# Attention and spectral mixing: the last mode groups moved between loop and tail, and the last sixteen modes scattered row by row

## The chip, the cores and the metric

The kernel runs on one core of a Trainium2 chip. The metric is device time in microseconds from launch to end, the median of several runs. The profile shows one execution of its own; the time from its first to its last instruction is called the span.

The engines are PE (matrix products and transposes), DVE (vector), ACT (scalar functions and copies), POOL (GpSimd) and SP (issues transfers). POOL and SP each have a queue of DMA transfers of their own, and both use the same 16 DMA engines.

## The reference

Inputs in float32: q, k, v of shape (8 batches, 8 heads, 576 positions, 64), w_phi (64 x 128), and for the second half w_r and w_i (64 modes x 512 x 512 each) and w_ch (512 x 512).

```python
# 1. linear attention with a Hedgehog feature map
def phi(x):
    proj = x @ w_phi
    proj = proj - max(abs(proj), axis=-1)
    return concat([exp(proj), exp(-proj)], axis=-1)
kv  = einsum('bhsf,bhsd->bhfd', phi(k), v)
z   = sum(phi(k), axis=2)
num = einsum('bhsf,bhfd->bhsd', phi(q), kv)
den = einsum('bhsf,bhf->bhs', phi(q), z) + 1e-06
x   = num / den                      # as (batch, position, head * 64 + d)
# 2. spectral mixing
X = rfft(x, axis=1)                  # the first 64 modes are used
Yr = Xr @ w_r - Xi @ w_i             # per mode m: (512) @ (512 x 512)
Yi = Xr @ w_i + Xi @ w_r
u = x + irfft(Y)
out = u + relu(u @ w_ch)
```

The 134 MB of w_r and w_i are read once and cast to bfloat16 on the way by the transfers themselves.

## The kernel before

**First part, a loop of 32 + 2 iterations (L577 to L654).** Iteration n works on stage n: two heads of one batch, or one head of two batches. It is a software pipeline: features and maxima of the current stage, key-value products `kv_mm` and numerators of the stage before, and `x_mm`, the forward Fourier transform as products with cosines and sines, of the stage before that. The result of the transform lies in XT0 or XT1. `vscale` (L278) multiplies V on POOL by exponentials `ee` that ACT makes from the maxima of this iteration. All of it is written in the order of issue by hand (`tc.manual_schedule()`), and each engine runs its own instructions in that order.

**The mode groups.** The products with w_r and w_i are split into 32 groups of 2 MB after the cast (`groups`, L108): a group k >= 8 is a quarter of the 512 input features (g = 1, 2, 3) and eight modes (gi = 0 to 7). Each has four loads of 512 KB, two of w_r and two of w_i, issued from POOL (L166). Three groups have buffers (`NW = 3`), so the loads of group k are issued after the products of group k-3. `weights(k)` puts the four issues on the list `due`, and `issue_weights(n)` takes up to n from it. In iterations 4 to 8 up to four loads are issued and V is scaled afterwards (before iteration 4, V comes first); from iteration 9 it scales V first and issues three, from 27 on four.

The list `at` (L548) says after which iteration `mode_mm` multiplies the next group: group 16 after iteration 27, 17 after 29, 18 after 30 and 19 after 31. `mode_sum` adds the group into Yacc at the start of the next iteration (L453), and for g = 3 into a bfloat16 tile `yst` (L462) instead.

**Second part, the tail (L816 to L851).** It begins with group 20. Beside the remaining groups it does for all pairs of blocks of x: `flip_x` (8 transposes on PE into PSUM tag T3, a copy sT on DVE) and `times_w` (products with w_ch, `psW`, tag T2, copied to xw on ACT), as the list `plan` spreads them by `pieces`. `reordered` puts rows of x in another order. For groups 24 to 31, the last input features, yst is transposed (ptY, tag T3) to sY, and after every second of them `by_batch` makes both z, the product of sY with w_ch, and the modes themselves with rows of one batch together: 64 products of 32 columns of sY into T0 and T1. ACT and DVE copy eight pieces of 32 rows to `zy`, whose halves are called zall and yall. For the last pair (groups 30 and 31) only batches 0 and 4 are copied directly; the other six go through a bfloat16 tile `st` and six transfers of 64 KB, two from SP and four from POOL.

**Third part, 20 output units (L873 to L888).** A unit is two blocks of 128 positions (four units are half as large). `add_xw` and `add_z` sum x w_ch and the inverse transform of z in a PSUM tile psB, ACT takes the Relu (L793); `add_x` and `spec` sum x and the inverse transform of the modes in psA, DVE adds the two (L807). For 11 units marked late, POOL adds x instead (L811). SP sends the result (L888). Units take the tags T2 and T3, or T0 and T1, in turn. The psB of the first unit is begun before group 31's products, its psA after group 31's transposes.

PSUM is claimed by tags: a tile of a tag waits until the readers of the tile before it in that tag are done.

Of the kernel before, what the change touches and what calls it, by code (L numbers as in the profile page):

```python
# [10 lines left out]
F32 = mybir.dt.float32  # L11
F32R = mybir.dt.float32r
BF16 = mybir.dt.bfloat16
# [13 lines left out]
def kernel(  # L27
# [379 lines left out]
                             start=(dc == 0), stop=(dc == 3))  # L407
        nc.scalar.copy(xw0[:, i, :], ps)

    def mode_mm(k, tag="yr"):  # L410
        g, gi = groups[k]
        XT = XTs[1 - g if k < 8 else g % 2]
        wt = W.pop(k)
        if gi < 0:
            psY = psum.tile([128, 2, DMODEL], F32, name="psY2", tag="pC", bufs=1)
            for par in range(2):
                for ri in range(2):
                    for j in range(4):
                        for x in range(2):
                            r = slice(64 * x, 64 * x + 64)  # L420
                            m = 16 * (-1 - gi) + 8 * x + 2 * j + par
                            c0 = (16, 0, 48, 32)[2 * ri + par]
                            nc.tensor.matmul(
                                psY[32 * j:32 * j + 32, x, :],
                                lhsT=XT[r, c0:c0 + 32, m],
                                rhs=wt[ri][r, 2 * j + par, :],
                                start=(par == 0 and ri == 0), stop=(par == 1 and ri == 1),
                            )
            return psY
        psY = psum.tile([128, DMODEL], F32, name="psY", tag=tag, bufs=1)  # L430
        for ri in range(2):
            for i in range(2):
                for j in range(4):
                    nc.tensor.matmul(  # L434
                        psY[32 * j:32 * j + 32, :],
                        lhsT=XT[:, 16 + 32 * ri:48 + 32 * ri, 32 * i + 4 * gi + j],
                        rhs=wt[ri][:, 2 * j + i, :],
                        start=(i == 0 and ri == 0), stop=(i == 1 and ri == 1),
                    )
        return psY  # L440

    def mode_sum(k, psY, pb=None):
        g, gi = groups[k]
        if gi < 0:
            G = -1 - gi
            if g == 0:
                nc.vector.tensor_copy(Yacc[:, 2 * G:2 * G + 2, :], psY)
            else:
                nc.vector.tensor_tensor(
                    out=Yacc[:, 2 * G:2 * G + 2, :], in0=psY, in1=Yacc[:, 2 * G:2 * G + 2, :],  # L450
                    op=ALU.add)
        elif g < 3:
            nc.vector.tensor_tensor(  # L453
                out=Yacc[:, gi, :], in0=psY, in1=Yacc[:, gi, :], op=ALU.add)
        else:

            cuts = [0, DMODEL] if k < 31 else [0, DMODEL // 2, DMODEL]
            yst = []
            for a, b in zip(cuts, cuts[1:]):
                t = pb.tile([128, b - a], BF16, name="yst", tag="yst" if k < 31 else f"yst{a}",  # L460
                            bufs=2 if k < 31 else 1)
                nc.vector.tensor_tensor(out=t, in0=psY[:, a:b], in1=Yacc[:, gi, a:b], op=ALU.add)  # L462
                yst += [t[:, x:x + 128] for x in range(0, b - a, 128)]
            return yst


# [78 lines left out]

    psY = None
    k_in = k_out = 0
    at = [5, 6, 7, 8, 9, 10, 12, 13, 17, 18, 19, 20, 21, 23, 24, 25, 27, 29, 30, 31]  # L548
    pa_last_cm = None
    with tc.manual_schedule():  # L550
        load(S[0], "qk")
# [25 lines left out]
        for n in range(N + 2):  # L577
# [110 lines left out]
        nc.vector.tensor_copy(sT, pt)  # L688
        ahead.append((i, sT))

    def times_w():
        i, sT = ahead.pop(0)
        ps = psum.tile([128, 2, DMODEL], F32, name="psW", tag="T2")
        for x in range(2):
            for dc in range(4):
                nc.tensor.matmul(ps[:, x, :], lhsT=sT[:, x, dc, :], rhs=wchb[:, dc, :],  # L696
                                 start=(dc == 0), stop=(dc == 3))
        nc.scalar.copy(xw[:, i - N_EARLY:i + 2 - N_EARLY, :], ps)  # L698

    def pieces(n):  # L700
        for _ in range(n):
            if todo:
                flip_x(todo.pop(0))
            if copies:
                copies.pop(0)()
            if len(ahead) > 1:
                times_w()
            if copies:
                copies.pop(0)()
# [18 lines left out]
    def by_batch(sY, P):  # L728
# [19 lines left out]
        def copy(j, h, eng):  # L748
            eng(zy[rows, :, j + 4 * h, :], ps[h][32 * j:32 * j + 32])

        if P < 3:
            for h in range(2):
                mm_z(h)
                mm_r(h)
            copies.extend([lambda j=j: (copy(j, 0, nc.scalar.copy),
                                        copy(j, 1, nc.vector.tensor_copy)) for j in range(4)])
            return

        for h, eng in ((0, nc.scalar.copy), (1, nc.vector.tensor_copy)):
            mm_z(h)
            mm_r(h)
            copy(0, h, eng)
            st = pb.tile([128, 2, DMODEL], BF16, name=f"st{h}", bufs=1)
            eng(st, ps[h])
            for j in range(1, 4):
                (nc.sync if j == 1 else nc.gpsimd).dma_start(
                    zy[rows, :, j + 4 * h, :], st[32 * j:32 * j + 32])

    def parts(u):
# [37 lines left out]
            nc.gpsimd.tensor_tensor(out=o, in0=o, in1=xs_all[:, i:i + 2, :], op=ALU.add)  # L811


    u0 = dict(bc=((0, 0), (0, 1)), half=False, late=False, tags=("T2", "T3"))

    with tc.manual_schedule():  # L816
        plan = {20: 3, 21: 3, 22: 2, 23: 2, 24: 1, 25: 1, 26: 1, 27: 1, 28: 1, 29: 1, 30: 1, 31: 0}
        while k_out < 32:
            k = k_out
            gi = groups[k][1]  # L820
            while k_in < min(k_out + NW, 32):
                weights(k_in)
                k_in += 1
            issue_weights()
            if k == 31:
                add_xw(u0)
            yst = mode_sum(k, mode_mm(k, "T3"), pb)
            k_out += 1
            if yst is not None:
                if ahead:  # L830
                    times_w()
                if gi % 2 == 0:
                    sY = pb.tile([128, 4, 2, 128], BF16, name="sY", tag="sY")
                for a, b, tag in ((0, 4, "T3"),) if k < 31 else ((0, 2, "T0"), (2, 4, "T1")):
                    pt = psum.tile([128, b - a, 128], BF16, name="ptY", tag=tag)
                    for dc in range(a, b):
                        nc.tensor.transpose(pt[:, dc - a, :], yst[dc], ident_b)
# [81 lines left out]
```

## Time and profile before

| what | value |
|---|---|
| time, median of 3 runs | 454.23 us (453.52 to 456.52) |
| time of the profiled execution | 453.88 us |
| its span | 452.1 us |
| PE, DVE, ACT, POOL busy | 314.2, 293.5, 270.1, 218.5 us |
| queue q0 (POOL) | 76.75 MB, 94.8% of 16 engines' span |
| queue q1 (SP and others) | 20.19 MB, 13.0% |
| read from and written to HBM | 163.64 MB, 9.44 MB |
| mean granted PE clock | 0.863 |

The page of the profile lists busy times, then the span in 40 slices of 11.3 us with the busy share in tenths, the DMA queues, the chain of work that ended last, the costliest groups of instructions, and the DMA issues. Other views give single instructions in order of time (start, duration, engine, line, operation, output <- inputs, count, and in brackets the idle time before and what ended it), or the busy time of each engine in chosen windows: after each window's length come five pairs of busy us and instructions (PE, weight loads of PE, DVE, ACT, POOL), then the granted PE clock, the busy share of the DMA engines and the GB/s that landed. PEld is the loading of PE's weights. The span is 1.8 us shorter than the same execution's time.

### The profile page before, as it was taken

What the parts mean: (1) busy time and instruction counts of PE and PEld (TensorE: products, weight loads), DVE (VectorE), ACT (ScalarE), POOL (GpSimd) and SP (SyncE); (2) the same over time, 40 slices, a digit from 0 to 9 for tenths busy, and PEclk for the clock granted to TensorE, in tenths of its full rate; (3) what the DMA queues carried; (4) which work ended last, traced back from release to release, by engine and by line L of the source; (5) the groups of instructions that cost most, each with busy time, mean ns of one, the idle gap of its engine ahead of it and who ended that gap; (6) DMA issues with size and microseconds to landing.
All of it is one profiled execution on the core that took longest, in us unless ns stands there. A gap on an engine that the chain in (4) does not pass through costs nothing.

```text
span 452.1 us, 11841 instructions
## 1 busy us (share of the span) xinstructions
PE 314.2 (69%) x4980; PEld 209.1 (46%) x4997; DVE 293.5 (65%) x418; ACT 270.1 (60%) x552; POOL 218.5 (48%) x303
## 2 busy tenths in 40 slices
PE   3475677677848777666858766665788868677993
PEld 2364465565626655444635644442444534243341
DVE  6578879987858788866756877752322263454873
ACT  4575787885746868765846866652344552353662
POOL 3955558394554744844535652460222322200893
PEclk9987989986676679988686789886999988799998
DMA  6999999999999999999999999999999999992697
GB/s 179 195 229 219 201 219 218 229 218 218 224 226 216 227 221 221 219 222 221 234 221 220 222 223 211 177 198 211 211 211 211 210 211 211 211 210 52 234 337 300
DMA packets 60612, 97.75 MB, mean 216 GB/s; under 512 B 3920, under 2 KB 28752, under 8 KB 60560
## 3 DMA queue, kind: packets, MB, share of 16 engines
q0 software_dynamic: 51920, 76.75, 94.8%
q1 hardware_dynamic: 8480, 20.19, 13.0%
q8 instruction: 39, 0.64, 0.5%
q14 instruction: 13, 0.11, 0.1%
q10 hardware_dynamic: 160, 0.07, 0.1%
HBM read 163.64 MB, written 9.44 MB: 383 GB/s over the span
## 4 chain that ended last, share of the span: by engine, by line
DMA 29%; PE 24%; DVE 22%; ACT 13%; issue 5%; POOL 5%; SPq 1%; DVEq 0%; ACTq 0%; POOLq 0%
DMA wi<-in_moe_w_i_dram 28%; DVE mkq L245 7%; DVE xs_all L348 4%; PE psW L696 4%; ACT AA L252 3%; DVE nd L334 3%; PE psY L434 3%; ACT e L274 2%; DVE tB L327 2%; PE psNB L317 2%; PE kvz L298 2%; ACT AA L256 2%; POOL vaug L282 2%; PE psWe L406 1%; ACT kvzF L307 1%
## 5 line engine op out<-in xcount | busy, mean ns | idle before, releaser
L282 POOL TENSOR_TENSOR vaug<-vn,ee 128x576 bf16<-128x576 f32 x64 | 72.8, 1158 | 99.8 <-ACT ee L267 94.5
L252 ACT ACTIVATE AA<-psT 128x1024 bf16<-128x1024 f32 x64 | 62.0, 1021 | 25.7 <-PE psT L220 25.1
L256 ACT ACTIVATE AA<-psk 128x1024 bf16<-128x1024 f32 x64 | 61.4, 1009 | 0.0
L274 ACT ACTIVATE e<-mkq 64x4 f32<-64x4 f32 (+1 forms) x128 | 26.3, 206 | 58.5 <-DVE mkq L245 56.1
L166 POOL DMA_DIRECT2D wr<-in_moe_w_r_dram x48 | 30.1, 633 | 57.9 <-PE psY L434 45.4
L698 ACT CAST xw<-psW 128x1024 bf16<-128x1024 f32 x17 | 17.2, 1012 | 48.3 <-PE psW L696 48.3
L166 POOL DMA_DIRECT2D wi<-in_moe_w_i_dram x48 | 30.3, 640 | 22.4 <-DMA wi<-in_moe_w_i_dram 12.9
L245 DVE TENSOR_REDUCE mkq<-psk 128x8 f32<-128x1024 f32 x32 | 38.8, 1213 | 3.2 <-PE psk L211 3.1
L245 DVE TENSOR_REDUCE mkq<-psq 128x8 f32<-128x1024 f32 x32 | 39.0, 1217 | 0.3
L696 PE MATMUL psW<-wchb,sT 128*128 128x512 bf16 x129 | 34.5, 406 | 4.5 <-ACT xw L698 3.4
L202 DVE COPY kT<-ptr 128x640 bf16<-128x640 bf16 x32 | 15.7, 492 | 29.9 <-PE ptr L196 29.9
L317 PEld LDWEIGHTS <-AA 128*128 128x128 bf16 x640 | 31.2, 115 | 8.3 <-issue 7.8
L298 PE MATMUL kvz<-vaug,AA 64*128 64x65 bf16 x1152 | 30.1, 213 | 5.3 <-POOL vaug L287 3.8
L434 PEld LDWEIGHTS <-XT 128*32 128x32 bf16 x384 | 16.1, 167 | 37.8 <-DMA wi<-in_moe_w_i_dram 18.9
L327 DVE TENSOR_TENSOR tB<-psNB,e 128x650 f32<-128x650 f32 x32 | 26.7, 834 | 10.4 <-PE psNB L317 9.6
L220 PE MATMUL psT<-qT,w 64*128 64x512 bf16 x64 | 15.0, 456 | 24.4 <-DVE mkq L245 24.3
L453 DVE TENSOR_TENSOR Yacc<-psY,Yacc 128x512 f32<-128x512 f32 x16 | 11.0, 689 | 31.9 <-PE psY L434 31.8
L298 PEld LDWEIGHTS <-AA 64*128 64x128 bf16 x1152 | 25.7, 109 | 9.8 <-issue 6.5
L348 DVE TENSOR_TENSOR xs_all<-nd,rden 128x640 bf16<-128x640 f32 x32 | 28.8, 900 | 1.1
L196 PE MATMUL ptr<-ident_b,k 128*128 128x128 bf16 x160 | 19.2, 271 | 14.6 <-DVE qT L202 11.3
L334 DVE TENSOR_TENSOR nd<-psNA,tB 128x650 f32<-128x650 f32 x32 | 26.7, 835 | 3.8 <-DVE tB L327 0.5
L434 PE MATMUL psY<-wi,XT 128*32 128x512 bf16 x192 | 17.8, 441 | 16.3 <-DMA wi<-in_moe_w_i_dram 16.3
(134 smaller groups left out, 737.9 us busy)
## 6 DMA issues: line engine op xcount, KB each, us to landing
wr<-in_moe_w_r_dram POOLq DMA_DIRECT2D x64, 512.0 KB, 13.6
wi<-in_moe_w_i_dram POOLq DMA_DIRECT2D x64, 512.0 KB, 15.2
out_dram<-of SPq DMA_DIRECT2D x16, 512.0 KB, 3.6
vn<-in_v_dram SPq DMA_DIRECT2D x24, 288.0 KB, 6.1
q<-in_q_dram POOLq DMA_DIRECT2D x12, 288.0 KB, 11.2
k<-in_k_dram POOLq DMA_DIRECT2D x12, 288.0 KB, 12.4
vn<-in_v_dram SPq DMA_DIRECT2D x16, 144.0 KB, 4.8
out_dram<-Yacc SPq DMA_DIRECT2D x8, 128.0 KB, 2.8
```

What stands on the lines that cost most here:

```text
L166: nc.gpsimd.dma_start(t.rearrange("p (m i) e -> p m (i e)", i=2), w[8 * gi + y:8 * gi + 8:2, g * 128:(g + 1) * 128, :].rearrange("m (p i) ...
L245: nc.vector.tensor_reduce(out=o, in_=i, axis=AX.X, op=ALU.max, apply_absolute_value=True)
L252: nc.scalar.activation(AA[:, 0, ab, 0:1024].rearrange("f (x j p) -> f j x p", j=2, p=64), st["psT"].rearrange("f j (x p) -> f j x p", p=64 ...
L256: nc.scalar.activation(AA[:, 1, ab, 0:1024].rearrange("p (c j f) -> p j c f", c=4, j=2), st["psk"], ACT.Exp, scale=sc)
L282: nc.gpsimd.tensor_tensor(out=vaug[:, ab, :, 0:64], in0=st["v"], in1=ee[:, ab, :].unsqueeze(2).to_broadcast([128, 9, D_]), op=ALU.mult,)
L298: nc.tensor.matmul(kvz[:, hh, ab * 65:(ab + 1) * 65], lhsT=AA[r, 1, ab, 128 * j:128 * j + 128], rhs=vaug[r, ab, j, :], start=(j == 0), sto ...
L317: nc.tensor.matmul(p[:, hh, 65 * c:65 * c + 65], lhsT=AA[:, 0, ab, x:x + 128], rhs=kvzF[:, hh, ab * 65:(ab + 1) * 65], start=True, stop=True,)
L327: nc.vector.tensor_tensor(out=tB, in0=st["psNB"], in1=e2.unsqueeze(3).to_broadcast([128, 2, NCH, 65]), op=ALU.mult,)
L334: nc.vector.tensor_tensor(out=nd, in0=st["psNA"], in1=st["tB"], op=ALU.add)
L348: nc.vector.tensor_tensor(out=xo, in0=nd[:, :, :, 0:64], in1=rden.to_broadcast([128, 2, NCH, 64]), op=ALU.mult,)
L434: nc.tensor.matmul(psY[32 * j:32 * j + 32, :], lhsT=XT[:, 16 + 32 * ri:48 + 32 * ri, 32 * i + 4 * gi + j], rhs=wt[ri][:, 2 * j + i, :], st ...
L696: nc.tensor.matmul(ps[:, x, :], lhsT=sT[:, x, dc, :], rhs=wchb[:, dc, :], start=(dc == 0), stop=(dc == 3))
```

## The change

Four things change together.

1. *Attachment.* Group 17 is multiplied after iteration 28, 18 after 29, 19 after 30, and group 20, formerly the first of the tail, after 31. The tail begins with group 21, and `plan` spreads its pieces over one group fewer.
2. *Order of issue.* From iteration 9 on, two loads are issued ahead of V's scaling and two behind it.
3. *The last sixteen modes.* `by_batch` serves the first three pairs only. For groups 30 and 31 `by_row` sends the rows of yst to yall and those of z to zall, seven batches by transfers of 16 rows (16 KB), two on SP and five on POOL each time. `z_of_group` makes z of one group with four products; `first_batch` makes batch 0 of both groups directly.
4. *Order at the end and PSUM tags.* The copies of the third pair are all issued in iteration 29 of the tail. Two `times_w` and the first unit's `add_x` stand between group 31's products with w_r and those with w_i; two flips without products stand behind group 30. The units use T2 and T1, or T0 and T3, so that T3 and T0 serve the last groups' products and are free again for the second unit.

```diff
-    at = [5, 6, 7, 8, 9, 10, 12, 13, 17, 18, 19, 20, 21, 23, 24, 25, 27, 29, 30, 31]
+    at = [5, 6, 7, 8, 9, 10, 12, 13, 17, 18, 19, 20, 21, 23, 24, 25, 27, 28, 29, 30, 31]
...
-            if 9 <= n < N:
-                vscale(cur)
...
-            issue_weights(3 if 9 <= n < 27 else 4)
+            issue_weights(4 if n < 9 else 2)
             if n in (1, 3):
                 load_qk((n + 5) // 2)
-            if 4 <= n < 9:
+            if 4 <= n < N:
                 vscale(cur)
+            if n >= 9:
+                issue_weights(2)
...
-    def pieces(n):
+    def pieces(n, keep=1):
...
-            if len(ahead) > 1:
+            if len(ahead) > keep:
                 times_w()
...
+    def by_row(all_b, t, gi):
+        for b in (4, 1, 5, 2, 6, 3, 7):
+            (nc.sync if b in (4, 1) else nc.gpsimd).dma_start(
+                all_b[16 * gi:16 * gi + 16, b, :], t[b::8, :])
+
+    def first_batch(sY):
+        cols = [sY[:, dc].rearrange("p g c -> p (g c)")[:, 0::8] for dc in range(4)]
+        ps = psum.tile([128, 2, DMODEL], F32, name="psZY", tag="T0")
+        r = slice(96, 128)
+        for dc in range(4):
+            nc.tensor.matmul(ps[r, 0, :], lhsT=cols[dc], rhs=wchb[:, dc, :],
+                             start=(dc == 0), stop=(dc == 3))
+        for dc in range(4):
+            nc.tensor.matmul(ps[r, 1, dc * 128:(dc + 1) * 128], lhsT=cols[dc], rhs=ident_b,
+                             start=True, stop=True)
+        nc.scalar.copy(zall[r, 0, :], ps[r, 0, :])
+        nc.vector.tensor_copy(yall[r, 0, :], ps[r, 1, :])
+
+    def z_of_group(sY, gi):
+        ps = psum.tile([128, DMODEL], F32, name="psZ", tag="T3")
+        for dc in range(4):
+            nc.tensor.matmul(ps, lhsT=sY[:, dc, gi % 2, :], rhs=wchb[:, dc, :],
+                             start=(dc == 0), stop=(dc == 3))
+        z = pb.tile([128, DMODEL], BF16, name="z8", tag="z8")
+        nc.scalar.copy(z[:, 0:256], ps[:, 0:256])
+        nc.vector.tensor_copy(z[:, 256:512], ps[:, 256:512])
+        by_row(zall, z, gi)
...
-        plan = {20: 3, 21: 3, 22: 2, 23: 2, 24: 1, 25: 1, 26: 1, 27: 1, 28: 1, 29: 1, 30: 1, 31: 0}
+        plan = {21: 3, 22: 3, 23: 2, 24: 2, 25: 1, 26: 1, 27: 1, 28: 1, 29: 1, 30: 2, 31: 0}
...
+            psY = mode_mm(k, "T3", ris=(0, 1) if k < 31 else (0,))
             if k == 31:
+                times_w("T2")
+                times_w("T0")
+                add_x(u0)
+                mode_mm(k, ris=(1,), psY=psY)
                 add_xw(u0)
-            yst = mode_sum(k, mode_mm(k, "T3"), pb)
+            yst = mode_sum(k, psY, pb)
             k_out += 1
             if yst is not None:
+                if gi >= 6:
+                    by_row(yall, yst, gi)
                 if ahead:
                     times_w()
...
-                if k == 31:
-                    add_x(u0)
-                if gi % 2 == 1:
+                if gi == 7:
+                    first_batch(sY)
+                if gi >= 6:
+                    z_of_group(sY, gi)
+                elif gi % 2 == 1:
                     by_batch(sY, gi // 2)
-            pieces(plan[k])
+            pieces(plan[k], 2 if k == 30 else 1)
+            while copies and k == 29:
+                copies.pop(0)()
...
-            if k == 30:
-                times_w()
...
-            u["tags"] = ("T2", "T3") if n % 2 == 0 else ("T0", "T1")
+            u["tags"] = ("T2", "T1") if n % 2 == 0 else ("T0", "T3")
```

More of the change, by code (lines that the diff above doesn't have):

```diff
@@ L408, in times_w_early, with mode_mm @@
         nc.scalar.copy(xw0[:, i, :], ps)
-    def mode_mm(k, tag="yr"):
+    def mode_mm(k, tag="yr", ris=(0, 1), psY=None):
         g, gi = groups[k]
         XT = XTs[1 - g if k < 8 else g % 2]
-        wt = W.pop(k)
+        wt = W[k]
         if gi < 0:
@@ L429, in mode_mm @@
             return psY
-        psY = psum.tile([128, DMODEL], F32, name="psY", tag=tag, bufs=1)
-        for ri in range(2):
+        if psY is None:
+            psY = psum.tile([128, DMODEL], F32, name="psY", tag=tag, bufs=1)
+        for ri in ris:
             for i in range(2):
@@ L455, in mode_sum @@
         else:
+            yst = pb.tile([128, DMODEL], BF16, name="yst", tag="yst", bufs=3)
             cuts = [0, DMODEL] if k < 31 else [0, DMODEL // 2, DMODEL]
-            yst = []
             for a, b in zip(cuts, cuts[1:]):
[L460 to L463, printed above, removed]
+                nc.vector.tensor_tensor(out=yst[:, a:b], in0=psY[:, a:b], in1=Yacc[:, gi, a:b],
+                                        op=ALU.add)
             return yst
@@ L689, in flip_x, with times_w @@
         ahead.append((i, sT))
-    def times_w():
+    def times_w(tag="T2"):
         i, sT = ahead.pop(0)
-        ps = psum.tile([128, 2, DMODEL], F32, name="psW", tag="T2")
+        ps = psum.tile([128, 2, DMODEL], F32, name="psW", tag=tag)
         for x in range(2):
@@ L749, in copy @@
             eng(zy[rows, :, j + 4 * h, :], ps[h][32 * j:32 * j + 32])
[L751 to L761, printed above, removed]
+        for h in range(2):
             mm_z(h)
             mm_r(h)
[L764 to L769, printed above, removed]
+        copies.extend([lambda j=j: (copy(j, 0, nc.scalar.copy),
+                                    copy(j, 1, nc.vector.tensor_copy)) for j in range(4)])
+    def by_row(all_b, t, gi):
[23 more added lines that the diff above has]
+        by_row(zall, z, gi)
     def parts(u):
@@ L811, in spec @@
             nc.gpsimd.tensor_tensor(out=o, in0=o, in1=xs_all[:, i:i + 2, :], op=ALU.add)
-    u0 = dict(bc=((0, 0), (0, 1)), half=False, late=False, tags=("T2", "T3"))
+    u0 = dict(bc=((0, 0), (0, 1)), half=False, late=False, tags=("T2", "T1"))
     with tc.manual_schedule():
-        plan = {20: 3, 21: 3, 22: 2, 23: 2, 24: 1, 25: 1, 26: 1, 27: 1, 28: 1, 29: 1, 30: 1, 31: 0}
+        plan = {21: 3, 22: 3, 23: 2, 24: 2, 25: 1, 26: 1, 27: 1, 28: 1, 29: 1, 30: 2, 31: 0}
         while k_out < 32:
@@ L833 @@
                     sY = pb.tile([128, 4, 2, 128], BF16, name="sY", tag="sY")
-                for a, b, tag in ((0, 4, "T3"),) if k < 31 else ((0, 2, "T0"), (2, 4, "T1")):
+                for a, b, tag in ((0, 4, "T3"),) if k < 31 else ((0, 2, "T0"), (2, 4, "T3")):
                     pt = psum.tile([128, b - a, 128], BF16, name="ptY", tag=tag)
                     for dc in range(a, b):
-                        nc.tensor.transpose(pt[:, dc - a, :], yst[dc], ident_b)
+                        nc.tensor.transpose(pt[:, dc - a, :], yst[:, dc * 128:(dc + 1) * 128],
+                                            ident_b)
                     nc.vector.tensor_copy(sY[:, a:b, gi % 2, :], pt)
-                if k == 31:
-                    add_x(u0)
-                if gi % 2 == 1:
+                if gi == 7:
[3 more added lines that the diff above has]
+                elif gi % 2 == 1:
                     by_batch(sY, gi // 2)
-            pieces(plan[k])
+            pieces(plan[k], 2 if k == 30 else 1)
+            while copies and k == 29:
+                copies.pop(0)()
             if k <= 24 or k % 2 == 0:
```

## The prediction

> **What bounds the kernel now.** I read first the page's slices, then the groups with their releasers, then windows where the slices dip, and last the timeline from the final weights on.
>
> ```profile
> DMA  6999999999999999999999999999999999992697
> ...
> q0 software_dynamic: 51920, 76.75, 94.8%
> ...
> wi<-in_moe_w_i_dram POOLq DMA_DIRECT2D x64, 512.0 KB, 15.2
> ```
>
> The 16 DMA engines are full from the second slice to the 36th, and GpSimd's queue (q0), which carries the weights, holds them for 94.8% of the span. So up to about 411 us the kernel is a stream of weights; an engine's work counts only if it delays a load, or comes after the last one. The stream has one real hole:
>
> ```profile
> core 0: us, PE busy (x) PEld busy (x) DVE busy (x) ACT busy (x) POOL busy (x), PEclk, DMA share, GB/s
> 282.00:284.00 2.00, 1.41 (x53) 1.19 (x50) 1.79 (x3) 1.89 (x3) 0.00 (x0) 1.00 1.12 210
> 284.00:286.00 2.00, 1.76 (x45) 1.51 (x43) 1.45 (x3) 1.98 (x6) 1.37 (x2) 1.00 1.05 199
> 286.00:288.00 2.00, 0.31 (x4) 0.31 (x3) 1.76 (x3) 1.62 (x5) 2.00 (x4) 0.93 0.59 114
> 288.00:290.00 2.00, 1.62 (x13) 0.78 (x13) 1.57 (x2) 0.00 (x0) 1.47 (x3) 0.50 0.86 137
> 290.00:292.00 2.00, 2.00 (x24) 0.78 (x24) 0.10 (x2) 1.41 (x5) 0.00 (x0) 0.72 1.07 197
> ...
> 298.00:300.00 2.00, 1.48 (x13) 0.94 (x14) 1.40 (x3) 0.09 (x1) 1.94 (x4) 0.50 1.12 164
> 300.00:302.00 2.00, 2.00 (x19) 0.77 (x17) 0.53 (x1) 1.28 (x5) 0.00 (x0) 0.66 1.05 188
> ```
>
> The last column is what landed; 211 GB/s is the steady rate of weights alone. In the timeline the first load that ends the hole is issued at 286.98, behind the scaling of V (L282), which had waited for ACT.
>
> After the last load, the timeline:
>
> ```profile
> 402.98 0.69 DVE L462 TENSOR_TENSOR yst<-psY,Yacc 128x512 bf16<-128x512 f32 x1
> ...
> 409.56 0.68 PE L434 MATMUL psY<-wr,XT 128*32 128x512 bf16 x8
> 411.45 0.69 PE L434 MATMUL psY<-wi,XT 128*32 128x512 bf16 x8 [1.21 <-DMA wi<-in_moe_w_i_dram]
> ...
> 418.50 1.22 DVE L807 TENSOR_TENSOR of<-psA,of 128x1024 f32<-128x1024 f32 x1
> ```
>
> For group 31 PE waits for the load, not the load for PE: everything that could be done before has been done by 411.45, with 1.2 us to spare. From there 40.7 us remain, nearly all of them the 20 output units; PE is busy 9.8 of 10 us in them, so they shift as a block with the moment at which they can run freely.
>
> **The change, part by part.** Starts and durations are those of the profiled execution (span 452.1, its own time 453.88, against a median of 454.23).
>
> *Attachment and order of issue.* Group 17's product moves from iteration 29 to 28, 18 to 29, 19 to 30, 20 from the tail to 31. A group's product frees the buffers of the group three later, so group 20's loads can be issued one iteration earlier, at about 272 to 277 instead of 286.98, and two of the four now stand before V's scaling, where POOL idles 5.07 to 6.91 us for ACT. The lost bytes are, window by window, (12+97+74+14+47+23) GB/s x 2 us = 534 KB, at 211 GB/s **2.5 us**. Bounds: 0, if the hole reappears elsewhere; 3.5, if the smaller dips before it go too. I take 2.5, the measured hole: the loads of 17, by the order of the stream, have landed when iteration 28 ends (the queue, filled up to the issue at 277.06, ran dry near 286; two groups of 10 us earlier is 266, iteration 28 ends at 270). The two issues cost 2 x 0.64 = 1.28 us of POOL per iteration, covered by that idle time; without the cover V's scaling would be 1.28 us later, and behind it wait the second pair of loads and the kv products, which had 3.4 us of room (copy of ee done at 259.2, first product at 262.56). An issue can also wait for an older load: rows of the tail show 1.6 to 2.2 us for each. That needs a full queue, so it delays compute but starves nothing. Cost taken: 0. Group 20's product (1.5 us of PE) and sum (0.69 us of DVE) enter iteration 31, beside the loads.
>
> *The last products after the last load.* Removed: by_batch for the last pair, 64 small matmuls (413.64 to 416.08, 2.4 us of PE), four evictions (1.0 and 1.0 on ACT, 1.22 and 1.23 on DVE) and six transfers of 64 KB. Added after the load: first_batch (4 products of 512 columns by 0.215 = 0.86, 4 of 128 columns about 0.25), z_of_group (4 x 0.215 = 0.86), evictions of half size, and 14 transfers of 16 KB, four on SP, ten on POOL (0.55 each, 5.5 us, done before POOL's first addition L811). From the start w of the last wi product: sums and transposes as before, second copy of sY done w+2.2, first_batch done w+3.4, its two evictions w+4.0, z half copies w+4.8, Relu of the first unit w+4.9 to 5.9, first L807 at w+5.9. Before, it was 418.50 - 411.45 = 7.05, because DVE was held by two evictions of 1.2 us. The third unit needs batch 4 by transfer: issued w+4.85 on SP, landing 2.1 us later (the median of the six st transfers; 1.9 to 2.2), w+7.0, a stall of 0.2 us. The second unit finds T0 and T3 free, where T0 and T1 had to wait for st. Net **-1.2 us**, bounds -1.5 and -0.4 (if rows of 16 KB land a microsecond later). The Trainium skill, "DMA: Bandwidth & Descriptors", section "Bandwidth", speaks against the split: transfers under 64 KB are dominated by descriptors and should be batched. By the fit under "Anatomy of one DMA" a 16 KB row would be estimated at 2.04 us against 2.15 for 64 KB, so the sum by it is the same to 0.1; the 64 KB rows here agree with 1.9 to 2.2 us.
>
> *Between the last two groups.* This is the term that I think decides. Before, group 30 did one flip and one product with w_ch; now its step holds the group's z product, two flips, then group 31's wr product, two products with w_ch and add_x, all in PE order ahead of the wi product. Let L be the landing of group 30's wi (401.0 before); 31's lands at L+10. All four pairs of copies of by_batch(2) now run in iteration 29. Before, two ran (400.50 to 402.95) and yst began at 402.98 = L+2.0. Two more of 1.22 put it at L+4.4; if the products of group 29 run at full clock (they ran at half: psW 3.6 instead of 1.9, psZY started late) some 2.3 us less, L+2.1. Then, strictly in turn between PE and DVE: yst 0.69, ptY 0.40, sY 0.42, z 1.0, its copy 0.42, flip 0.61, sT 0.69, flip 0.61, sT 0.69, nine hand-overs of 0.05: 6.0. Then wr 0.5, two psW of 8 x 0.215 = 1.73 back to back, add_x 0.43: 4.4. The wi product starts at L+12.5 to L+14.8 at full clock, **2.5 to 4.8 us after its load**, where before it was 0. T0 and T2 are ready by then. On top comes the clock. The views by windows show what follows a thin one:
>
> ```profile
> 366.22:369.63 3.41, 1.28 (x15) 0.89 (x15) 2.21 (x4) 3.02 (x3) 1.05 (x2) 1.00 1.12 210
> 369.63:373.04 3.41, 2.44 (x16) 0.68 (x18) 1.46 (x2) 1.85 (x2) 0.79 (x2) 0.50 1.12 211
> ...
> 386.70:390.11 3.41, 1.21 (x10) 0.36 (x9) 2.81 (x3) 1.95 (x2) 0.87 (x2) 1.00 1.12 210
> 390.11:393.52 3.41, 2.44 (x12) 0.84 (x13) 0.69 (x1) 0.00 (x0) 0.61 (x1) 0.50 1.12 211
> ```
>
> PE busy 1.2 or 1.3 us of 3.41 was followed by a granted clock of 0.50 for two windows. The alternation above has PE busy 0.40 + 1.0 + 0.61 in about 5 us, as thin; the two psW would then take up to 7 us for 3.5. Bounds: 2.5 (early, full clock) and 9.0 (late, and 4.2 for products at half clock). I take **+5.1**: between the two full-clock ends (3.6), and about a third of what the clock can add (1.5), because a half-clock group 29 leaves the next step no idle time and so a full clock at its start. The Trainium skill, "TensorE: Matmul & The Clock Gate", Part 1, says that the clock falls after at least one idle window of about 3.4 us. Read strictly it would not fall here, and the sum would be 1.5 lower, 453.8. This trace is against that strict reading: 1.21 us busy sufficed.
>
> **Sum:** -2.5 + 5.1 - 1.2 = +1.4; 453.88 + 1.4 = **455.3 us**.
>
> **Rivals.**
> 1. *Full clock through the last two groups.* Wait 2.5 to 4.8, middle 3.6: -2.5 + 3.6 - 1.2, 453.8 us (452.7 to 455.0). For it: 400.35 to 414 ran at full clock. Against it: the new order thins PE there. It is also what the page on the clock gate gives when read strictly.
> 2. *Nothing of it binds.* If group 30's chain is overtaken by nothing and the two psW fit into the wait for the load, as they are placed, the whole gain stays: 453.88 - 2.5 - 1.2 = 450.2 us. For it: PE had 1.2 us spare at 411.45. Against it: the chain above is longer than the 10 us between two groups.
> 3. *Slower: half clock over both psW.* The wait becomes 9.0 and the first units start cold: -2.5 + 9.0 - 1.2 = +5.3, 459.2 us. It decides from a wait of 3.7 on, since below that the gains outweigh it. For it: the thin windows above; against it: PE has to fall cold exactly in that step.
> 4. *The loop doesn't do what it says.* POOL waits before V's scaling for older loads, kv products slip, the hole moves: 0 gained, 5.1 lost, 1.2 gained, 457.8 us. For it: POOL waited 9.6 us for loads at L166 before 270 already; against it: those waits come with a full queue.
>
> **How the numbers follow.** Forecast, half clock for part of that step, 0.42 (waits from 4 to 8, 454.2 to 458.2); rival 1 0.24, rival 2 0.08, rival 3 0.17, rival 4 0.09. The range 451.0 to 459.8 leaves out rival 2 and the upper half of rival 3. About 1% is what a measurement of this kernel can tell from no change: 449.7 to 458.8. Below lies a part of rival 2, 0.06; above most of rival 3 and the upper edges of rival 4 and the forecast, 0.21; within, 0.73.
>
> **What would show it.** Right: no window under 200 GB/s between 284 and 302; loads end near 409; the last wi product starts several us after its load, released by PE's own order, with PE thin in the 6 us behind group 30's psW and perhaps a clock of 0.50; first L807 some 5.9 us after that product. Wrong: a last wi product released by its load (rival 2), a new hole (rival 4), or L807 still 7 us behind.

## The result and the profile after

| | before | after |
| --- | --- | --- |
| median of the runs | 455.65 us (453.52 to 457.96, 22 runs) | 459.05 us (455.87 to 461.63, 22 runs) |
| ratio after to before | | 1.0066, 95% interval 1.0048 to 1.0085 |
| profiled execution, its span | 453.88 us, 452.1 us | 456.75 us, 454.8 us |

The change makes the kernel slower by 0.66%, which is 3.0 us (2.2 to 3.9). A ratio here is formed from the runs themselves and is not the quotient of the two medians: these lie 3.4 us apart, the means (458.56 and 455.57) 3.0. The forecast had +1.4 us. Both profiled executions lie under the mean of their runs, that of before by 1.7 us and that of the changed kernel by 1.8, so the two traces together show nearly the whole loss, 2.9 us.

The page of the changed kernel, the lines that answer to those of before (its line numbers are those of the changed file):

```profile
span 454.8 us, 11804 instructions
...
DMA  6999999999999999999999999999999999990597
...
q0 software_dynamic: 52432, 76.82, 93.9%
...
wi<-in_moe_w_i_dram POOLq DMA_DIRECT2D x64, 512.0 KB, 19.0
```

The first row has no digit under 9 from the second slice to the 36th, as before, and q0 holds 93.9% against 94.8%. The loads of w_i now take 19.0 us from issue to landing instead of 15.2: they are issued earlier and wait longer in a fuller queue. None of this shows where 2.7 us of span were added. For the hole, the windows of 2 us (columns as before: the granted clock, the DMA share and GB/s are the last three):

```profile
core 0: us, PE busy (x) PEld busy (x) DVE busy (x) ACT busy (x) POOL busy (x), PEclk, DMA share, GB/s
...
284.00:286.00 2.00, 2.00 (x19) 0.72 (x17) 0.41 (x1) 1.40 (x5) 0.00 (x0) 0.60 1.12 211
286.00:288.00 2.00, 1.75 (x45) 1.02 (x39) 1.63 (x2) 1.04 (x3) 1.22 (x2) 1.00 1.12 211
288.00:290.00 2.00, 1.55 (x61) 1.47 (x54) 1.47 (x5) 1.98 (x5) 0.52 (x1) 1.00 1.12 211
...
298.00:300.00 2.00, 0.87 (x18) 0.87 (x18) 0.27 (x2) 1.98 (x5) 0.60 (x1) 0.81 1.12 211
300.00:302.00 2.00, 1.53 (x26) 1.31 (x24) 1.83 (x4) 2.00 (x5) 2.00 (x4) 0.50 1.12 211
```

The last column is at 211 where it was 199, 114, 137, 164 and 188, and no window from 282 to 302 is under 209. The hole is closed, as forecast. The end of the weights, in the timeline of the changed kernel:

```profile
400.02 0.67 PE L435 MATMUL psY<-wi,XT 128*32 128x512 bf16 x8 [1.62 <-DMA wi<-in_moe_w_i_dram]
...
402.66 0.69 DVE L461 TENSOR_TENSOR yst<-psY,Yacc 128x512 bf16<-128x512 f32 x1
...
406.29 0.61 PE L684 MATMUL pt<-ident_b,xs_all 128*128 128x128 bf16 x8 [0.92 <-DVE z L781]
...
409.06 1.09 PE L435 MATMUL psY<-wr,XT 128*32 128x512 bf16 x8 [0.78 <-DVE sT L687]
...
410.08 4.50 PE L695 MATMUL psW<-wchb,sT 128*128 128x512 bf16 x15
410.17 1.44 POOL L758 DMA_DIRECT2D zy<-z  x3 [2.13 <-DMA wi<-in_moe_w_i_dram]
...
414.94 0.69 PE L435 MATMUL psY<-wi,XT 128*32 128x512 bf16 x8
...
420.65 1.23 DVE L819 TENSOR_TENSOR of<-psA,of 128x1024 f32<-128x1024 f32 x1 [0.66 <-DMA zy<-yst]
```

Before, the last product with w_i was released by its load, at 411.45. Now it starts at 414.94 and names no DMA. The last weights have landed at about 410.15: there POOL, which waited for one of them before it could issue a row transfer, goes on (410.17, releaser wi). In the kernel with the step made short, further down, POOL goes on 0.13 us after the product that the load itself releases, so this mark is good to about 0.2 us. So the loads end 1.3 us earlier than before, and the product comes 4.8 us after them. From that product to the first addition of an output unit it is now 420.65 - 414.94 = 5.7 us instead of 7.05, and from the product to the end of the span 39.9 us instead of 40.65, so 0.8 less. -1.3 + 4.8 - 0.8 is +2.7, and the span grew by 2.7.

The windows of that step in the changed kernel (columns as in the windows above):

```profile
402.00:404.00 2.00, 0.92 (x7) 0.26 (x5) 1.48 (x3) 1.01 (x1) 0.00 (x0) 1.00 1.13 213
404.00:406.00 2.00, 1.04 (x4) 0.41 (x5) 0.46 (x2) 0.37 (x1) 1.94 (x4) 1.00 0.91 174
406.00:408.00 2.00, 0.93 (x14) 0.81 (x14) 0.92 (x2) 0.00 (x0) 1.46 (x4) 1.00 0.64 128
408.00:410.00 2.00, 1.22 (x14) 0.46 (x10) 0.69 (x1) 0.00 (x0) 0.03 (x1) 0.62 0.54 116
410.00:412.00 2.00, 2.00 (x9) 0.74 (x6) 0.00 (x0) 0.00 (x0) 1.44 (x3) 0.53 0.06 16
412.00:414.00 2.00, 1.95 (x10) 0.89 (x10) 0.00 (x0) 1.01 (x1) 0.00 (x0) 1.00 0.03 8
```

From 402 to 408 PE is busy about half of the time (0.92, 1.04 and 0.93 of each 2 us, the second number of a row), and then the granted clock falls, to 0.62 and 0.53; from 412 it is 1.00 again. The product with w_r (409.06) and the first of the two products with w_ch (from 410.08) run in it: w_r's takes 1.09 us instead of 0.68, and the 15 recorded matmuls with w_ch take 4.50 us.

### The profile page after: what moved, and what is told of

The parts are those of the page before. It is cut to its first block, busy times and chain, and to the rows that moved or that the text cites. A ratio compares the mean times of both kernels' runs of the same rounds, so it can differ in the third digit from the quotient of the medians.

```text
span 454.8 us, 11804 instructions
## 1 busy us (share of the span) xinstructions
PE 310.1 (68%) x4932; PEld 207.2 (46%) x4949; DVE 297.2 (65%) x419; ACT 270.2 (59%) x553; POOL 227.9 (50%) x319
## 3 DMA queue, kind: packets, MB, share of 16 engines
q0 software_dynamic: 52432, 76.82, 93.9%
## 4 chain that ended last, share of the span: by engine, by line
PE 30%; DMA 22%; DVE 20%; ACT 13%; POOL 6%; issue 6%; SPq 1%; DVEq 0%; ACTq 0%; POOLq 0%
DMA wr<-in_moe_w_r_dram 8%; DMA wi<-in_moe_w_i_dram 8%; PE psW L695 6%; DMA q<-in_q_dram 5%; ACT AA L252 4%; DVE mkq L245 4%; PE psY L435 4%; DVE xs_all L348 3%; DVE zy L748 3%; DVE nd L334 3%; POOL vaug L282 2%; ACT AA L256 2%; PE psNB L317 2%; PE psWe L406 2%; PE pt L684 2%
## 5 line engine op out<-in xcount | busy, mean ns | idle before, releaser
L298 PE MATMUL kvz<-vaug,AA 64*128 64x65 bf16 x1152 | 28.2, 206 | 23.3 <-POOL vaug L287 20.7
L695 PE MATMUL psW<-wchb,sT 128*128 128x512 bf16 x127 | 32.4, 391 | 3.2 <-ACT xw L697 2.7
L348 DVE TENSOR_TENSOR xs_all<-nd,rden 128x640 bf16<-128x640 f32 x32 | 32.8, 1024 | 1.1
L687 DVE COPY sT<-pt 128x1024 bf16<-128x1024 bf16 x17 | 11.8, 692 | 23.1 <-PE pt L684 23.1
L435 PE MATMUL psY<-wr,XT 128*32 128x512 bf16 x192 | 18.9, 473 | 10.6 <-ACT AA L260 5.3
```

Source lines behind the costliest of these rows:

```text
L298: nc.tensor.matmul(kvz[:, hh, ab * 65:(ab + 1) * 65], lhsT=AA[r, 1, ab, 128 * j:128 * j + 128], rhs=vaug[r, ab, j, :], start=(j == 0), sto ...
L348: nc.vector.tensor_tensor(out=xo, in0=nd[:, :, :, 0:64], in1=rden.to_broadcast([128, 2, NCH, 64]), op=ALU.mult,)
L435: nc.tensor.matmul(psY[32 * j:32 * j + 32, :], lhsT=XT[:, 16 + 32 * ri:48 + 32 * ri, 32 * i + 4 * gi + j], rhs=wt[ri][:, 2 * j + i, :], st ...
```

## The experiments

Each is compared with the kernel before, run on the same chip; the medians of before were 455.4 to 455.7 us. Ratios have 95% intervals.

### The loop's two edits alone

The tail as before, with one pair of blocks more after group 25, since group 20 has left the tail.

```diff
-    at = [..., 24, 25, 27, 29, 30, 31]
+    at = [..., 24, 25, 27, 28, 29, 30, 31]
...
-            if 9 <= n < N:
-                vscale(cur)
...
-            issue_weights(3 if 9 <= n < 27 else 4)
+            issue_weights(4 if n < 9 else 2)
...
-            if 4 <= n < 9:
+            if 4 <= n < N:
                 vscale(cur)
+            if n >= 9:
+                issue_weights(2)
...
-        plan = {20: 3, 21: 3, 22: 2, 23: 2, 24: 1, 25: 1, ...
+        plan = {21: 3, 22: 3, 23: 2, 24: 2, 25: 2, ...
```

> The kernel before with the new attachment and the new order of issue in the loop, and the tail as it was (17 pairs of blocks, one more behind group 25). Theory A (the loop's part gives a little, the tail's step between groups 30 and 31 takes more): the last load lands about 1 us earlier than before, the last wi product is still released by its load, 452.5 to 454 us where before has 454 to 455.5, ratio 0.996 to 0.999. Theory B (the loss sits in the loop: POOL is blocked ahead of V's scaling): as slow as the whole change, ratio 1.004 to 1.009. Theory C (the hole of 534 KB was all lost time): -2.5 us, ratio 0.994. Also: if the 16 engines drift apart once the hole is gone, the landed rate falls off over some 5 us at the end here too; if the row transfers did that, it falls off over 2 us as before.

Measured: 452.99 us, ratio 0.9946 (0.9920 to 0.9972), that is -2.5 us (-1.2 to -3.6). That is theory C, and the forecast's first term is there at its full size in the timed runs. In its profiled execution (span 452.6) the last product with w_i starts at 410.29, released by its load, so 1.16 us earlier than before; the first L807 comes only 8.64 us later, and there the granted clock had fallen to 0.51 (412 to 414). This execution, 454.63 us, lies 1.6 us above the median and shows less of the gain.

### The tail's edits alone

The changed kernel with `at` and the order of issue as before, and `plan` for twelve groups again.

```diff
-        plan = {21: 3, 22: 3, 23: 2, 24: 2, 25: 1, 26: 1, ..., 30: 2, 31: 0}
+        plan = {20: 2, 21: 3, 22: 2, 23: 2, 24: 1, 25: 1, 26: 1, ..., 30: 2, 31: 0}
```

> The changed kernel with the loop as before (attachment and order of issue), group 20 again the first of the tail. Theory A: loads land as before (near 411.4), the last wi product 4 to 6 us later than its load, gain of about 0.8 in the output units, so +3.5 to +5 us, ratio 1.008 to 1.011. Theory B: the tail's part is a gain, ratio 0.995 to 1.000.

Measured: 459.82 us, ratio 1.0100 (1.0067 to 1.0133), +4.6 us. So the tail costs more than the loop gives. The timeline of its last groups:

```profile
401.69 4.92 DVE L748 CAST zy<-psZY 32x1024 bf16<-32x1024 f32 x4
...
406.64 0.69 DVE L461 TENSOR_TENSOR yst<-psY,Yacc 128x512 bf16<-128x512 f32 x1
...
415.87 4.52 PE L695 MATMUL psW<-wchb,sT 128*128 128x512 bf16 x16
...
420.76 0.69 PE L435 MATMUL psY<-wi,XT 128*32 128x512 bf16 x8
```

DVE copies all four pieces of the third pair first (4.92 us), the sum yst of group 30 waits until 406.64, the product with w_r and the first part of those with w_ch run at a half clock (granted clock 0.50 from 408 to 416, 0.57 from 416 to 418), and the last product with w_i comes at 420.76. What landed falls from 184 GB/s in 408 to 410 to 44 in 412 to 414, so its load was there by about 412: some 9 us of wait, rival 3's case, in one execution. That execution, 462.54 us, is the highest of seven, 2.7 us above their median, so this wait need not be the usual one.

### Only the issue order, only the attachment

The two halves of the loop's edits, each by itself in the kernel before. The order:

```diff
-            if 9 <= n < N:
-                vscale(cur)
...
-            issue_weights(3 if 9 <= n < 27 else 4)
+            issue_weights(4 if n < 9 else 2)
...
-            if 4 <= n < 9:
+            if 4 <= n < N:
                 vscale(cur)
+            if n >= 9:
+                issue_weights(2)
```

The attachment:

```diff
-    at = [..., 24, 25, 27, 29, 30, 31]
+    at = [..., 24, 25, 27, 28, 29, 30, 31]
...
-        plan = {20: 3, 21: 3, 22: 2, 23: 2, 24: 1, 25: 1, ...
+        plan = {21: 3, 22: 3, 23: 2, 24: 2, 25: 2, ...
```

> The kernel before with the new order of issue alone (four loads an iteration from iteration 9, two ahead of V's scaling), attachment as before. Theory A (the gain of e1 comes from group 17's earlier product, which lets loads be issued earlier): the hole near 285 us stays, though later or shorter, ratio 0.998 to 1.001. Theory B (the order makes the gain): 0.994 to 0.996.

> The kernel before with the new attachment alone (and the tail's plan that goes with it), loads issued behind V's scaling, three an iteration up to iteration 26. Theory A: the hole near 285 us is gone or nearly so, ratio 0.994 to 0.997, most of e1's gain. Theory B (attachment does nothing without the order): 0.998 to 1.001.

Measured: the order alone 458.79 us, ratio 1.0057 (1.0027 to 1.0086), slower; the attachment alone 452.96 us, ratio 0.9941 (0.9916 to 0.9966), the same as both together. The first is outside both of its theories, neither of which had more than 1.001; the second is inside theory A. So the loop's whole gain comes from the attachment, and the new order of issue adds nothing beside it that stands out of some 1.6 us of uncertainty, and harms without it. Why it harms is seen in the groups of instructions, first of before, then with the new order alone (idle time of POOL ahead of these issues, by what ended it):

```profile
L166 POOL DMA_DIRECT2D wr<-in_moe_w_r_dram x48 | 30.1, 633 | 57.9 <-PE psY L434 45.4 <-DMA wr<-in_moe_w_r_dram 6.9 <-DMA wi<-in_moe_w_i_dram 4.4
```

```profile
L166 POOL DMA_DIRECT2D wr<-in_moe_w_r_dram x48 | 29.8, 625 | 95.4 <-PE psY L434 56.8 <-DMA wi<-in_moe_w_i_dram 21.8 <-DMA wr<-in_moe_w_r_dram 7.8
```

The waits for older w_i loads rise from 4.4 to 21.8 us. They now stand ahead of V's scaling, and the loop's computation slips: the last scaling of V starts at 299.13 instead of 295.09, and group 17's product with w_r, after iteration 29, at 283.68 instead of 279.64, each 4.04 us later. A product frees the buffers for the next loads, so the stream runs dry for longer. What landed in the 40 slices, first before and then with the new order alone:

```profile
GB/s 179 195 229 219 201 219 218 229 218 218 224 226 216 227 221 221 219 222 221 234 221 220 222 223 211 177 198 211 211 211 211 210 211 211 211 210 52 234 337 300
```

```profile
GB/s 179 195 229 222 217 189 218 229 218 218 215 223 220 226 228 232 221 222 221 221 233 219 223 223 201 195 190 186 188 191 199 211 211 211 211 210 22 222 339 298
```

From the 25th to the 31st slice it is 186 to 201, where before only the 26th and 27th were under 211 (177 and 198), and the last load arrives 4.66 us later than before (416.11) in this execution, which lies 1.6 us above the median. In the changed kernel the same waits exist (16.8 us for w_i) and the last scaling of V is as late (299.39), but there group 17's product, now after iteration 28, starts at 274.27, buffers come free an iteration earlier and the slip is covered.

The attachment alone, its last product with w_i and its first output additions:

```profile
409.02 0.69 PE L434 MATMUL psY<-wi,XT 128*32 128x512 bf16 x8 [1.10 <-DMA wi<-in_moe_w_i_dram]
...
416.09 2.35 DVE L807 TENSOR_TENSOR of<-psA,of 128x1024 f32<-128x1024 f32 x2
```

409.02 is 2.43 us before 411.45, and from there it is 7.07 us, as before.

### The pairs earlier, no products with w_ch at the end

```diff
-        plan = {21: 3, ..., 25: 1, 26: 1, 27: 1, 28: 1, 29: 1, 30: 2, 31: 0}
+        plan = {21: 3, ..., 25: 2, 26: 2, 27: 1, 28: 1, 29: 1, 30: 0, 31: 0}
...
-                times_w("T2")
-                times_w("T0")
                 add_x(u0)
```

> The changed kernel, but the two pairs of blocks of groups 30 and 31 are flipped and multiplied behind groups 25 and 26 instead, so that no times_w stands ahead of the last wi product. Theory A: the last wi product starts within 0.5 us of its load, everything behind it comes 4 to 5 us sooner than in the changed kernel: 449.5 to 451 us on the clock of the profile, ratio to before 0.988 to 0.994. Theory B (the row transfers, not the order, hold up the end): no more than 1 us sooner than the changed kernel, ratio 1.003 to 1.007.

Measured: 452.77 us, ratio 0.9944 (0.9914 to 0.9975). Taking the two flips and the two products with w_ch out of the last step turns +0.66% into -0.56%, a little less than theory A had. The timeline shows that what is left of the step still does not fit:

```profile
400.82 4.93 DVE L748 CAST zy<-psZY 32x1024 bf16<-32x1024 f32 x4
...
405.78 0.69 DVE L461 TENSOR_TENSOR yst<-psY,Yacc 128x512 bf16<-128x512 f32 x1
...
410.46 1.09 PE L435 MATMUL psY<-wr,XT 128*32 128x512 bf16 x8 [0.92 <-DVE z L781]
...
412.45 1.10 PE L435 MATMUL psY<-wi,XT 128*32 128x512 bf16 x8
```

yst is again held back by four copies on DVE, and both products of group 31 run at a half clock (1.1 us instead of 0.68; the granted clock is 0.50 from 406 to 416). The first output addition, at 419.43, comes 7.0 us after the product instead of 5.7.

### PE kept busy in the last step

Eighteen products of 512 columns with the identity, whose result nobody reads, stand in PE's idle places of group 30's step. The first entry is a single execution, the second the same kernel timed.

```diff
+    def filler(k, n):
+        if k != 30:
+            return
+        ...
+            nc.tensor.matmul(fill_ps[0][:, 0, :], lhsT=ident_b, rhs=wchb[:, 0, :],
+                             start=True, stop=True)
...
                 flip_x(todo.pop(0))
+                filler(k_out - 1, 4)
...
+                filler(k, 4)
                 if gi % 2 == 0:
...
+                filler(k, 2)
...
                     z_of_group(sY, gi)
+                    filler(k, 4)
```

> The changed kernel with 18 idle products of 512 columns (0.215 us each, into a PSUM tile nobody reads) in the gaps of PE in group 30's step, so that the clock can't fall. If the half clock is part of the 4.8 us: the two psW of group 31 together take 3.6 instead of 4.5 us, wr 0.68 instead of 1.09, and the last wi product starts 3 to 4 us after its load. If the clock has no share: 4.5 to 5 us after it, the fillers only being in the way.

> The same kernel as e4, now timed: the changed kernel with 18 idle products in PE's gaps of group 30's step. If the half clock in that step is what makes the changed kernel's median worse than its profiled execution: ratio 0.996 to 1.001, that is 2.5 to 4.5 us better than the changed kernel's 1.0066. If the clock has little share: 1.003 to 1.007.

Measured: the single execution 453.83 us, with the last product with w_i at 412.38; the timed kernel 455.58 us, ratio 0.9991 (0.9966 to 1.0015). The windows and the timeline of the timed kernel:

```profile
404.00:406.00 2.00, 1.94 (x16) 1.03 (x14) 0.82 (x2) 0.37 (x1) 1.69 (x4) 1.00 0.70 139
406.00:408.00 2.00, 2.00 (x18) 1.09 (x20) 0.99 (x2) 0.00 (x0) 0.48 (x1) 1.00 0.56 118
408.00:410.00 2.00, 1.84 (x15) 0.81 (x13) 0.00 (x0) 0.00 (x0) 0.89 (x2) 1.00 0.12 28
```

```profile
401.34 0.69 DVE L461 TENSOR_TENSOR yst<-psY,Yacc 128x512 bf16<-128x512 f32 x1
...
407.75 0.69 PE L435 MATMUL psY<-wr,XT 128*32 128x512 bf16 x8
...
408.60 3.40 PE L695 MATMUL psW<-wchb,sT 128*128 128x512 bf16 x15 [0.16 <-issue]
409.11 1.44 POOL L759 DMA_DIRECT2D zy<-z  x3 [2.17 <-DMA wi<-in_moe_w_i_dram]
...
412.36 0.69 PE L435 MATMUL psY<-wi,XT 128*32 128x512 bf16 x8
...
418.06 1.23 DVE L820 TENSOR_TENSOR of<-psA,of 128x1024 f32<-128x1024 f32 x1 [0.66 <-ACT of L806]
```

PE is busy throughout, and the granted clock stays at 1.00. From yst to the product with w_r it takes 6.4 us in both kernels, so the idle products delay nothing; from there to the last product with w_i it takes 4.6 us instead of 5.9. The same 15 matmuls take 3.40 us, and the product comes 3.25 us behind its load (409.11 to 412.36): the lateness of the order of work alone, without the clock. More work on PE makes the kernel faster: 1.0066 against 0.9991 is 0.75%, about 3.4 us. The traces put 1.55 us of that (4.8 - 3.25) on the half clock; where the rest of the gain comes from they do not show.

### The step made short

Two of the third pair's copies go from DVE to ACT, one flip and one product with w_ch move ahead of the last two groups, and nine idle products keep PE busy (`filler` again, three behind the flip, two and four as above; not shown below).

```diff
-                                    copy(j, 1, nc.vector.tensor_copy)) for j in range(4)])
+                                    copy(j, 1, nc.scalar.copy if P == 2 and j > 1
+                                         else nc.vector.tensor_copy)) for j in range(4)])
...
-        plan = {21: 3, ..., 25: 1, 26: 1, ..., 30: 2, 31: 0}
+        plan = {21: 3, ..., 25: 2, 26: 1, ..., 30: 1, 31: 0}
...
                 times_w("T2")
-                times_w("T0")
                 add_x(u0)
```

> The changed kernel with one pair of blocks moved from group 30 to group 25, so that one times_w is left ahead of the last wi product; two of the four DVE copies of by_batch(2) given to ACT; and 9 idle products of 512 columns in PE's gaps in group 30's step, so that the clock stays up. Theory A (order, DVE copies and half clock together make the lateness): the last wi product is released by its load again, the first addition of an output unit comes 5.7 us after it, ratio to before 0.986 to 0.992. Theory B (something else holds the end, the row transfers for one): no better than e1 and e3, 0.994 to 0.997.

Measured: 451.28 us, ratio 0.9886 (0.9847 to 0.9925), faster than both kernels. The timeline of its end:

```profile
409.99 0.27 PEld L435 LDWEIGHTS <-XT 128*32 128x32 bf16 x8 [0.42 <-DMA wi<-in_moe_w_i_dram]
...
415.69 1.22 DVE L821 TENSOR_TENSOR of<-psA,of 128x1024 f32<-128x1024 f32 x1 [0.66 <-ACT of L807]
```

The weights of PE for the last product are released by the load of w_i again; nothing of the step is left behind it, and the first output addition still follows 5.7 us later. By these ratios the tail's edits carry a gain of their own once the step fits, 0.9886 against 0.9946 for the loop's edits alone; the two intervals just overlap.

### The same without idle products, and with the old order of issue

Against the kernel just shown, the first leaves out every `filler`; the second puts the order of issue back:

```diff
+            if 9 <= n < N:
+                vscale(cur)
...
-            issue_weights(4 if n < 9 else 2)
+            issue_weights(3 if 9 <= n < 27 else 4)
...
-            if 4 <= n < N:
+            if 4 <= n < 9:
                 vscale(cur)
-            if n >= 9:
-                issue_weights(2)
```

> The arrangement that beat both kernels (two more copies of the third pair on ACT, one flip and one product with w_ch fewer in the last step), now without the nine idle products that kept PE busy. Theory A, that the lateness of the last product came from the order of the work and the clock only added to it: with so much taken out of the step the last product with w_i stays released by its load or is at most 1.5 us late, even if the granted clock falls to 0.50; median 451 to 453.5, ratio 0.989 to 0.995. Theory B, that the idle products did the work: the clock falls, the last product comes 2 us or more behind its load and the median is 453.5 to 455, ratio 0.995 to 0.999.

> The arrangement that beat both kernels, with the order of issue as before (V scaled first, then three or four loads) and only the attachment new. Theory A, that the new order of issue adds nothing once the groups are attached one iteration earlier: median 450.5 to 452.5, ratio 0.987 to 0.993, as with the new order (451.28 and 0.9886). Theory B, that issuing two loads ahead of V's scaling is worth something of its own: 453 or more, ratio above 0.993.

Measured: without idle products 452.44 us, ratio 0.9949 (0.9924 to 0.9975); with the old order 451.89 us, ratio 0.9910 (0.9878 to 0.9942). The first falls between its theories: the median lies on the edge of both, and the timeline has the mechanism of the second one,

```profile
407.77 1.09 PE L435 MATMUL psY<-wr,XT 128*32 128x512 bf16 x8 [0.78 <-DVE sT L687]
...
408.80 2.98 PE L695 MATMUL psW<-wchb,sT 128*128 128x512 bf16 x8
...
410.06 1.44 POOL L759 DMA_DIRECT2D zy<-z  x3 [2.09 <-DMA wi<-in_moe_w_i_dram]
...
412.14 0.69 PE L435 MATMUL psY<-wi,XT 128*32 128x512 bf16 x8
```

w_r's product and the one product with w_ch at a half clock (1.09 and 2.98 us instead of 0.67 and 1.90), and the last product 2.1 us after its load. Short of work as the step is, the clock alone brings back a wait, and with it the tail's own gain is gone: 0.9949 is what the loop's edits have alone. In the second kernel the order of issue shows no worth of its own either, as far as intervals of plus or minus 1.5 us and more can tell. In its profiled execution (span 448.3, the shortest of all, and 1.8 us under the median of its runs) the last product with w_i starts at 408.41, released by its load, 3 us earlier than before, and the first output addition comes 5.7 us later. Its interval holds 0.9886.

## Why the prediction was right or wrong

*Direction and mechanism: right, size too small.* The hole closes, the chain of group 30's step sets the last product with w_i, this product is no longer released by its load, and the output units start sooner behind it. All four show in the trace, and the experiments separate them: loop alone -2.5 us, tail alone +4.6 us. The time, 459.05 us, lies in the forecast's range but 3.75 us above its 455.3. About 1.8 of that is the start: the sum began at the profiled 453.88, and the median of 22 runs of the kernel before is 455.65. The rest is the sum, +1.4 where the ratio has +3.0 and the medians 3.4. By time alone rival 3's 459.2 is nearer; from 455.65 it would be 461.0, and the wait in the trace is the forecast's (4.8 us) and not rival 3's (9.0).

*First term, -2.5: right in the timed runs, -1.3 in the profiled execution.* The loop's edits alone gave -2.5 us and the attachment alone -2.7 (0.9941). The profiled execution of the changed kernel showed half of that, because it lost bytes elsewhere. What landed from 60 to 70 us, first after and then before:

```profile
DMA packets 1551, 1.77 MB, mean 177 GB/s; under 512 B 76, under 2 KB 1422, under 8 KB 1550
```

```profile
DMA packets 1853, 2.08 MB, mean 208 GB/s; under 512 B 88, under 2 KB 1724, under 8 KB 1852
```

1.77 against 2.08 MB is 0.31 MB, 1.5 us at 211 GB/s. The loads there are issued by lines that the change leaves alone, but their moment differs, again first after and then before:

```profile
64.23 1.42 POOL L172 DMA_DIRECT2D wr<-in_moe_w_r_dram  x2 [3.40 <-PE psY L423]
```

```profile
62.92 1.43 POOL L172 DMA_DIRECT2D wr<-in_moe_w_r_dram  x2 [1.75 <-PE psY L423]
```

POOL issued them 1.3 us later because it waited for a group's product on PE, whose granted clock was 0.50 from 58 to 62 us; before, it was 0.75 and then 1.00. The same goes together in three more traces, those of the loop alone, of the order alone and of the short step without idle products: clock 0.50 from 58 to 62, issue at 63.88 to 64.56, 1.74 to 1.87 MB. The other eight traces, before among them, have a clock of 0.75 or more there, or 0.50 only until 60, the issue at 60.63 to 63.58 and 2.02 to 2.20 MB. Why the clock falls there in some executions and not in others was not tried.

*Second term, +5.1: 4.8 in the profiled execution, more by the timed runs.* It was 3.6 for the order of the work and 1.5 for the clock, "about a third of what the clock can add". The traces agree with both parts: the product is 3.25 us late with PE kept busy and 4.8 without, which leaves 1.55 for the clock. There is luck in this, since the reason given for the small share did not apply: it was a group 29 at half clock, and in this trace group 29's product with w_ch took 1.95 us, as at full clock, yst began 2.6 us after group 30's load, and the clock fell only after 408. The timed runs ask for more. The tail alone, +4.6 (3.1 to 6.1), makes the term 5.8 if the third is -1.2; the whole change makes it 3.0 + 2.5 + 1.2 = 6.7. The idle products gained 3.4 us (by the two intervals 2.0 to 4.8), and in the short step, 0.9886 against 0.9949, 0.63% or 2.9 us. If all of this is the clock, its 1.5 is what the sum had too small. That is not shown: the spans of the traces with and without the eighteen idle products differ by 2.6 us, and only 1.55 of that is the wait; 1.04 is that the loads end at 409.11 instead of 410.15, and the dip at 64 us, long before the idle products, lies in one of the two traces only. So in the traces the first term is the one that fell short, in the timed runs the second; the runs here leave open how the missing 1.6 us divide.

The Trainium skill, "TensorE: Matmul & The Clock Gate", Part 1, lets the clock fall after at least one idle window of about 3.4 us. Taken as a stretch without any product, that is not what was measured: from 402 to 408 the longest idle time ahead of a matmul is 0.92 us (the flip at 406.29), and the clock fell. Where PE's idle places were filled it did not.

*Third term, -1.2: -0.8 in the profiled execution.* The first output addition came at w+5.7, as forecast (5.9). The trace names a row transfer as what ended DVE's wait before it (420.65), but in the kernels with idle products, where ACT is named, it is 5.7 too, so the row transfers cost no stall of their own there. The rows behind the last product landed in 1.7 to 2.6 us (medians by tile and queue), where the forecast had 2.1. With the step made short, tail and loop together beat the loop alone by 0.6%, which is 2.7 us, though the intervals (0.9847 to 0.9925 and 0.9920 to 0.9972) just overlap; how much of that is this term stays open.

*Rivals.* Rival 1, a full clock, is what the kernel with idle products made true: forecast at 453.8 on 453.88, so no change, and measured at 0.9991. Rival 2, that nothing binds, is what the short step made true: forecast at -3.7 us, measured at 0.9886, which is -5.2 (-3.4 to -7.0). Rival 3's wait of 9 us came in the one trace of the tail alone. Rival 4 was right about a thing that the forecast put at a cost of 0: POOL does wait for loads ahead of V's scaling and the computation does slip, by 4 us; the cost was 0 because the attachment covers it, and 0.57% without.

## What to carry to other kernels

Work moved ahead of the last load is free only while the whole chain between the last two loads, hand-overs included, is shorter than their distance; count that chain before moving anything into it. A chain that alternates between engines can leave PE half idle, and then the clock must be priced for the matmuls behind it: here keeping PE busy with useless products gained 0.75%. One profile can lie 2 us from the middle of its runs, more than most terms of such a sum; set it against timed variants before a term is called right or wrong.

## What the runs showed of the hardware

The end of a stream has a width. The mean busy share of the 16 DMA engines from 400 to 416 us (slices of 0.4 us, tenths), first before and then after:

```profile
DMA  9999999999999999999999644310000000001000
```

```profile
DMA  9999999999998886767566543000111000000000
```

With the hole in it, the stream falls from full to nothing in about 2 us; with the hole closed it takes about 5. The attachment alone, where the last transfers by rows do not exist, takes more than 4 (404.0 to 408.4); the tail alone and the order alone, which keep a hole, take about 3. One reading is that the engines drift apart over a long stream and a hole lets the slow ones catch up; it is argued, not shown, and its cost is unknown. The Trainium skill, "DMA: Bandwidth & Descriptors", section "Latency and other measured facts", names engines 7 and 15 as usually slower in traces; no run here shows which engines are late.

A second finding is the dip at 64 us above: four of the twelve traces have it, in lines that are the same in all kernels and each time behind a granted clock of 0.50, and it makes a difference of 1.5 us between two traces that no edit was shown to cause. A half clock early in a kernel may thus cost the stream of loads, where a product decides when buffers come free.
